# Dummy products placed by the planner, and instruction fetches planned behind the queued data

## The chip, the cores and the metric

The kernel runs on one core of a Trainium2 chip. The metric is the device time of one execution in microseconds (us). PE is TensorE, DVE is VectorE, ACT is ScalarE, POOL is GpSimd, and SP is the engine that issues the loads and stores.

## The reference

Three layers follow each other, in float32. The first is attention in chunks: 4 batches of 8 heads, 768 positions, head size 64. A chunk of 32 queries sees 8 memory keys and the keys of its own chunk, of 16 positions to the left and of 8 to the right. The result, as 3072 tokens of 512 values, goes through two dense blocks:

```python
h = x @ w_in                      # 512 -> 2048
g = h * np.clip(h + 3.0, 0.0, 6.0) / 6.0
x = g @ w_out                     # 2048 -> 512
h = x @ w2_in
g = np.maximum(0.01 * h, h)
out = g @ w2_out
```

## The kernel before

Every dense product is made of three PE products of rounded parts (high times high, high times low, low times high). Weights arrive as 64-bit words; ACT and DVE decode each one into a high and a low part (`decode`, `split_w`), some 3 us of DVE for a weight tile. The tokens are worked on in blocks of 512. The first block is made of attention units: two whole units of 384 tokens (`unit(0, 0)` in the PSUM tile `at`, `unit(0, 1)` in `ab`) and two half units of 192 tokens (`half_unit(1, 0)` in two banks `h`, `half_unit(1, 1)` in `ac`). A unit is a chain: load q, k and v (SP) - windows of k copied (ACT, DVE or POOL) - `scores` (PE, L549 and L816) - `greatest` (DVE) - `exp` (ACT) - `total`, `norm` (DVE) - `transpose` (PE, L607 and L871) - `take_p` (ACT) - `values` (PE, L627, L639, L887, L899; for the first units also behind `memory`, a POOL copy of the memory rows in v) - `hi_x` (ACT) and `lo_x` (DVE), which write the high and low part of the block's `xh` and `xl`. When all four chains have written `xh`, the first dense product (L1003) can start.

The order of the work on each engine is written at build time by a planner, `schedule`. Each piece of work is a `Task` with a key (lower is more urgent), durations by engine, the tasks that it follows, and the tiles that it takes (`allocs`) or uses. The planner steps through a time of its own: whenever an engine is free it takes the most urgent task that is ready there, and emits its instructions. On the chip every engine runs its instructions in that order, each waiting for the data that it needs. The planner also prices loads (issue, start, rate, `LANDS` until the landing is seen, `SURE` as a margin) and, in `feed`, PE's instruction fetch: so many instructions held at the start (`HELD` = 447), so many more by each fetch (`FETCHED` = 256), `FETCH` after it is asked for.

Before the first dense product PE has little to do. `warm` adds tasks of dummy products, `ident` times `ident` (L466), at nine fixed points of the attention: two at the start, then one to three after certain `scores`, `transpose` and `values` tasks. They write the tile `ac`, from 512 columns wide at first to 256 columns later, where `ac` is at the same time the home of the second half unit.

Of the kernel before, what the change touches and what calls it, by code (L numbers as in the profile page):

```python
# [23 lines left out]
QK = 2 * G + 2 * KW  # L24
RAW = QK + 2 * D
NC = G // CHUNK
# [9 lines left out]
N = 512  # L36
# [18 lines left out]
PLAN += [(150 + 12 * k, "2i", k, 430 + 10 * k) for k in range(8)] + [(250 + 12 * k, "2o", k, 520 + 6 * k) for k in range(8)]  # L55
ROOMY = (3, 4, 5)
SOON = 15
RATE_QK, RATE, RATE_V, COLD = 380.0, 220.0, 300.0, 1.1
LOADS = ((-150, -149, -146, -144), (-148, -147, -142, -140), (-145, -138), (-143, -137), (-120, -118), (-116, -114))
WEIGHTS = (-141, -139, -136, -135, -134, -133, -115, -113, -112, -111, -110, -109)  # L60
SHIFT, SHIFT_HALF = (0,), (0,)
# [7 lines left out]
class Task:  # L69


    def __init__(self, fn, opts, key, after=(), allocs=(), uses=(), moe=False, issues=1, late=0, loads=False, ins=8):
        self.late, self.loads, self.ins = late, loads, ins
        self.fn, self.opts, self.key, self.moe, self.issues = fn, opts, key, moe, issues
        self.allocs, self.next, self.left, self.ready = allocs, [], 0, 0.0
        self.bufs = list(allocs) + list(uses)
        self.taken = False
        for b in self.bufs:
            b.users += 1
        for t in after:  # L80
            t.next.append(self)
            self.left += 1
# [9 lines left out]
QUEUED = 6000.0  # L92
LANES = 8
ISSUE = {"SP": 500.0, "POOL": 1000.0}
STARTS, LANDS, SURE = 1900.0, 500.0, 1500.0
HELD, FETCHED, FETCH, STALL = 447, 256, 5000.0, 250.0
AHEAD = 60
OTHER = 20
SLACK = 2500.0
# [1 line left out]
MARGIN = 300.0  # L101


def schedule(tasks, places, ends):

# [4 lines left out]
    future = []  # L112
    events, n, progress, now, wire = [], 0, 0, 0.0, 0.0
    lanes = {e: [0.0] * LANES for e in ISSUE}
    queue = (0, HELD, None)

    def feed(at, task):
        used, held, comes = queue
        for _ in range(task.ins):
            if comes is not None and comes <= at:  # L120
                held, comes = held + FETCHED, None
            if comes is None and used >= held - FETCHED:
                comes = at + FETCH
            if used >= held:
                at, held, comes = comes, held + FETCHED, None
            used += 1
            at += task.opts["PE"] / task.ins
        return at, (used, held, comes)
# [28 lines left out]
                    offer(t)  # L157

    def finish(task, e):
        for b in task.bufs:  # L160
            b.users -= 1
            if b.users == 0:
                live[b.tag].remove(b)
                for w in waiting[b.tag]:
                    offer(w)
                waiting[b.tag].clear()
        for t in task.next:
            if e == "PE" and e in t.opts:
                continue
            t.left -= 1  # L170
            if not t.left:
                push(now + (MARGIN if "PE" in t.opts and not t.moe else 0.0), "ready", t)
# [5 lines left out]
    while events:  # L178
# [10 lines left out]
        while again:  # L189
            again = False  # L190
            for e, h in heaps.items():
# [30 lines left out]
                for item in held:  # L222
                    heapq.heappush(h, item)
                if pick is None:
                    continue
                pick.taken = True
                for b in pick.allocs:
                    live[b.tag].append(b)
                pick.fn(e)
# [6 lines left out]
                if e == "SP" or pick.loads:  # L236
                    at = now
                    for _ in range(pick.issues):
                        at = max(at, lanes[e].pop(0)) + ISSUE[e]
                        wire = max(wire, at + STARTS) + d / pick.issues  # L240
                        lanes[e].append(wire + LANDS)
                    free[e] = at if pick.loads else max(at, wire - QUEUED)
                    push(free[e], "free", None)
                    push(wire + LANDS + (SURE if pick.allocs else 0.0), "done", (pick, e))
                    continue
                if e == "PE":
                    end, queue = feed(now, pick)
# [9 lines left out]
def tile_attn_moe_moe2(ctx: ExitStack, tc: tile.TileContext, raw, w1i, w1o, w2i, w2o, out):  # L257
# [196 lines left out]
    def made(b):  # L454
        return b.t if b.t is not None else make(b)

    marks = {}

    def warm(n, after=None, home=None):

        b, c = home or Buf("ac"), 2 if home else 4

        def fn(e):
            x = made(b)[:, 1, N - 128 * c:].rearrange("p (a n) -> p a n", a=c)
            for _ in range(n):
                nc.tensor.matmul(x, ident, ident.unsqueeze(1).to_broadcast([128, c, 128]), start=True, stop=True, skip_group_check=True)  # L466

        add(fn, {"PE": c * n * (220.0 if after else 430.0)}, after.key + 0.5 if after else -200.0, after=[after] if after else [], allocs=[] if home else [b], uses=[home] if home else [], ins=4 * n)

    def unit(j, quad, key, tag, own=False, direct=False, loads=None):  # L470

# [250 lines left out]
        l2 = [add(load_whole(i) if plain else load_v(i), {"SP": dma(128 * 2 * NC * 512, RATE_V if plain else RATE)}, loads[2 + i], after=() if own else t, allocs=[v[i]], issues=3 if plain else 6, loads=plain) for i in range(2)]  # L722
        if plain:
            l2 = [add(memory(i), {"POOL": 1500.0}, key - 20, after=[l2[i]], uses=[v[i]]) for i in range(2)]
        t = marks["s", j, quad] = add(scores, {"PE": (COLD if direct else 1.0) * 1300.0}, key - 16, ins=192, after=t, allocs=[ps], uses=[*qk, *kw])
        scored = t
        if direct and quad in SHIFT:
            t = add(greatest, {"DVE": 2100.0}, key - 15, after=[t], allocs=[mx, e], uses=[ps])
            t = add(exp_all, {"ACT": act(2 * PAIRS * W)}, key - 13, after=[t], uses=[e])
            t = add(total, {"DVE": 1250.0}, key - 12, after=[t], allocs=[s], uses=[e])  # L730
        else:
            t = add(greatest, {"DVE": 1200.0}, key - 15, after=[t], allocs=[mx], uses=[ps])
            t = add(exp(0), {"ACT": 6 * 330.0}, key - 13, after=[t], allocs=[e, s], uses=[ps, mx])
            if not own:
                turn[:] = [scored] if roomy else [t, *l2]
            t = add(exp(1), {"ACT": 6 * 330.0}, key - 13, after=[t], uses=[ps, mx, e, s])
            t = add(total, {"DVE": 350.0}, key - 12, after=[t], uses=[s])
        t = add(norm, {"DVE": 900.0} if direct else {"POOL": 1800.0, "DVE": 900.0}, key - 11, after=[t], uses=[e, s])
        t = marks["t", j, quad] = add(transpose, {"PE": (COLD if direct else 1.0) * 600.0}, key - 7, ins=12, after=[t], uses=[e, ps])
        t = add(take_p, {"ACT": act(PAIRS * 128)}, key - 5, after=[t], uses=[pt, e])  # L740
        t = marks["v", j, quad] = add(values_whole if plain else values, {"PE": (COLD if direct else 1.0) * 1600.0}, key, ins=192, after=[t, *l2], uses=[e, *v, ps])
        if jb >= PLAIN:
            to_pair(t, key, 0, NU)
            return
# [9 lines left out]
    def half_unit(j, quad, gp, key, tag, loads, copies, cold):  # L754
# [192 lines left out]
            if not blk:  # L947
                behind[:] = [a1]

        l1 = add(load_qk, {"SP": dma(128 * 2 * QK * 4, RATE_QK)}, loads[0], allocs=[qk])  # L950
        l2 = add(load_v, {"SP": dma(128 * 2 * NC * 512, RATE_V)}, loads[1], allocs=[v], issues=4 if whole else 8, loads=not gp)
        if whole:
            l2 = add(memory, {"POOL": 1500.0}, key - 20, after=[l2], uses=[v])
        t = add(windows, {copies: {"ACT": 1050.0, "DVE": 700.0, "POOL": 1800.0}[copies]}, key - 30, after=[l1], allocs=[kw], uses=[qk])
        t = marks["s", j, quad, gp] = add(scores, {"PE": cold * 650.0}, key - 16, ins=96, after=[t], allocs=banks, uses=[qk, kw])
        marks["b", j, quad, gp] = banks
        if gp or quad not in SHIFT_HALF:
            t = add(greatest, {"DVE": 700.0}, key - 15, after=[t], allocs=[mx], uses=banks)
            t = add(exp, {"ACT": 6 * 330.0}, key - 13, after=[t], allocs=[e, s], uses=[*banks, mx])
            t = add(total, {"DVE": 350.0}, key - 12, after=[t], uses=[s])  # L960
        else:
            t = add(greatest, {"DVE": 1250.0}, key - 15, after=[t], allocs=[mx, e], uses=banks)
            t = add(exp_all, {"ACT": act(2 * NC * W)}, key - 13, after=[t], uses=[e])
            t = add(total, {"DVE": 800.0}, key - 12, after=[t], allocs=[s], uses=[e])
        t = add(norm, {"DVE": 500.0}, key - 11, after=[t], uses=[e, s])
        t = marks["t", j, quad, gp] = add(transpose, {"PE": cold * 300.0}, key - 7, ins=6, after=[t], uses=[e, *banks])
        t = add(take_p, {"ACT": act(NC * 128)}, key - 5, after=[t], uses=[*banks, e])
        t = marks["v", j, quad, gp] = add(values_whole if whole else values, {"PE": cold * 900.0}, key, ins=96, after=[t, l2], uses=[e, v, *banks])
        jb, at = divmod(begins, N)
        first = min(2 * G, N - at)  # L970
        to_x(jb, t, key, at, 0, first)
# [590 lines left out]
        unit(0, u, -80.0 + 6.0 * u, ("at", "ab")[u], own=True, direct=True, loads=LOADS[u])  # L1562
    for u in range(2):
        half_unit(1, u, 0, -68.0 + 6.0 * u, ("h", "ac")[u], LOADS[2 + u], ("POOL", "DVE")[u], COLD)
    warm(2)
    warm(1, marks["s", 0, 0])
    warm(2, marks["s", 0, 1])
    warm(1, marks["s", 1, 0, 0])
    home = marks["b", 1, 1, 0][0]
    for m, n in ((("s", 1, 1, 0), 2), (("t", 0, 0), 3), (("t", 0, 1), 3), (("t", 1, 1, 0), 2), (("v", 1, 0, 0), 2)):  # L1570
        warm(n, marks[m], home)
    for u in range(2):
        half_unit(1, u, 1, -20.0 + 6.0 * u, "at", LOADS[4 + u], "ACT", 1.0)
    for u in range(2):
# [62 lines left out]

    with tc.manual_schedule():
        constants()
        schedule(tasks, places, ends)  # L1640

# [49 lines left out]
```

## Time and profile before

| what | value |
|---|---|
| time, median of 3 runs | 1047.82 us (1047.02 to 1048.76) |
| time of the profiled execution | 1049.14 us |
| its span, first to last instruction | 1047.4 us |
| mean granted clock of PE over the span | 0.992 of full |

The span is the stretch that the trace covers; the execution's own time holds 1.7 us more around it. Granted clock 1.00 is PE at 2.4 GHz, 0.50 is 1.2 GHz.

### The profile page before, as it was taken

Reading aid. Unit: us, or ns where it says so; the run is one execution under the profiler, and the core shown is the slowest. Engines: PE = TensorE matmul, PEld = TensorE weight load, DVE = VectorE, ACT = ScalarE, POOL = GpSimd, SP = SyncE. Lnnn points to the kernel's source line nnn. Section 1 sums busy time; section 2 is a strip of 40 time slices with the busy share of each in tenths; the row PEclk is TensorE's granted clock in tenths of the full one; section 3 lists DMA queues with packets and bytes.
Section 4 is the critical chain, followed back from the end, with each engine's and each line's share of the span. In section 5 each row is a group of like instructions: output and inputs, shape, how many; then the busy total and the mean of one; then the engine's idle time right before and its main releaser. Section 6 shows DMA issues by size and latency. Waiting matters only on the chain.

```text
span 1047.4 us, 20225 instructions
## 1 busy us (share of the span) xinstructions
PE 1035.1 (99%) x7476; PEld 850.3 (81%) x7476; DVE 875.3 (84%) x1485; ACT 693.7 (66%) x1480; POOL 20.8 (2%) x30
## 2 busy tenths in 40 slices
PE   7999999999999999999999999999999999999998
PEld 4778988888788888888888888888888888888886
DVE  6898988778998778799999899999576998566775
ACT  4786876655888555476686576785565874666753
POOL 3010000000000000000000000000000000000000
PEclk8899999999999999999999999999999999999999
DMA  9889787876887979673648778546342454423451
GB/s 265 283 216 331 241 291 230 258 229 221 262 282 239 332 225 290 239 239 123 214 144 268 253 251 280 183 158 221 111 171 81 174 193 156 173 109 96 146 181 61
DMA packets 127314, 220.49 MB, mean 211 GB/s; under 512 B 12528, under 2 KB 76016, under 8 KB 127216
## 3 DMA queue, kind: packets, MB, share of 16 engines
q1 hardware_dynamic: 127216, 219.20, 63.9%
q8 instruction: 59, 0.97, 0.4%
q14 instruction: 39, 0.32, 0.1%
HBM read 156.24 MB, written 62.91 MB: 209 GB/s over the span
## 4 chain that ended last, share of the span: by engine, by line
PE 89%; DVE 4%; DMA 3%; ACT 3%; issue 1%; SPq 0%; DVEq 0%; ACTq 0%
PE y L1327 15%; PE y L1052 13%; PE y L1495 12%; PE h L1327 10%; PE h L1495 8%; PE hx L1495 8%; PE h L1003 7%; PE hx L1327 7%; PE h L1052 2%; PE at L639 2%; DMA w<-in_raw 2%; PE at L549 1%; DVE w L345 1%; PE at L607 1%; PE ac L466 1%
## 5 line engine op out<-in xcount | busy, mean ns | idle before, releaser
L345 DVE TENSOR_TENSOR w<-w 128x512 fp32r<-128x512 f32 (+2 forms) x393 | 322.9, 854 | 25.8 <-ACT w L342 23.9
L342 ACT CAST w<-w 128x512 fp32r<-128x512 f32 (+1 forms) x290 | 223.3, 803 | 13.4 <-PE hx L1495 3.6
L1052 PE MATMUL y<-g,w 128*128 128x512 f32 (+1 forms) x540 | 125.2, 375 | 0.9 <-ACT g L342 0.7
L1327 PE MATMUL y<-w 128*128 128x512 f32 x516 | 124.6, 390 | 0.0
L1327 PEld LDWEIGHTS y<-w 128*128 128x128 f32 x516 | 96.6, 188 | 20.1
L1052 PEld LDWEIGHTS y<-g,w 128*128 128x128 f32 x540 | 94.1, 189 | 19.0 <-ACT g L342 1.2
L342 ACT CAST g<-w 128x512 fp32r<-128x512 f32 x80 | 49.4, 620 | 63.8 <-PE y L1495 23.0
L1495 PE MATMUL y<-w 128*128 128x512 f32 x384 | 90.3, 389 | 0.0
L1495 PEld LDWEIGHTS y<-w 128*128 128x128 f32 x384 | 72.1, 188 | 14.9
L1301 ACT ACTIVATE w<-w 128x512 f32<-128x512 f32 x72 | 45.0, 630 | 40.4 <-DVE w L1372 18.1
L1003 PE MATMUL h<-xh,w 128*128 128x512 f32 (+1 forms) x288 | 66.1, 370 | 0.5 <-DVE w L345 0.5
L345 DVE TENSOR_TENSOR g<-w,g 128x512 fp32r<-128x512 f32 x80 | 54.1, 684 | 14.3 <-ACT g L342 14.2
L1495 PE MATMUL h<-w 128*128 128x512 f32 x264 | 62.1, 389 | 0.0
L1495 PE MATMUL hx<-w 128*128 128x512 f32 x252 | 59.2, 389 | 0.0
L1327 PE MATMUL h<-xl,w 128*128 128x512 f32 x240 | 58.3, 391 | 0.0
L1495 PEld LDWEIGHTS h<-w 128*128 128x128 f32 x264 | 49.6, 188 | 10.3
L1003 PEld LDWEIGHTS h<-xh,w 128*128 128x128 f32 x288 | 49.7, 189 | 9.9 <-DVE w L345 0.9
L1495 PEld LDWEIGHTS hx<-w 128*128 128x128 f32 x252 | 47.3, 188 | 9.8
L1327 PEld LDWEIGHTS h<-xl,w 128*128 128x128 f32 x240 | 44.8, 188 | 9.9 <-DVE xl L345 0.4
L1327 PE MATMUL y<-xh,w 128*128 128x512 f32 x216 | 52.2, 390 | 0.0
L1327 PEld LDWEIGHTS y<-xh,w 128*128 128x128 f32 x216 | 40.5, 188 | 8.4
L1052 PE MATMUL y<-w 128*128 128x512 f32 x180 | 46.6, 391 | 0.0
(244 smaller groups left out, 1852.2 us busy)
## 6 DMA issues: line engine op xcount, KB each, us to landing
w<-kept2i SPq DMA_DIRECT2D x42, 512.0 KB
w<-kept2o SPq DMA_DIRECT2D x42, 512.0 KB
w<-kept1i SPq DMA_DIRECT2D x28, 512.0 KB
a<-in_raw SPq DMA_DIRECT2D x20, 448.0 KB
w<-in_w1i SPq DMA_DIRECT2D x16, 512.0 KB
w<-in_w1o SPq DMA_DIRECT2D x16, 512.0 KB
w<-in_w2i SPq DMA_DIRECT2D x16, 512.0 KB
w<-in_w2o SPq DMA_DIRECT2D x16, 512.0 KB
```

Source lines behind the costliest of these rows:

```text
L342: nc.scalar.copy(out, in_) if e == "ACT" else engine(e).tensor_copy(out=out, in_=in_)
L345: engine(e).tensor_tensor(out=out, in0=a, in1=b, op=ALU.subtract)
L466: nc.tensor.matmul(x, ident, ident.unsqueeze(1).to_broadcast([128, c, 128]), start=True, stop=True, skip_group_check=True)
L549: nc.tensor.matmul(ps.t[h * CHUNK:(h + 1) * CHUNK, par, i * W:(i + 1) * W], qk[h // 2].t[r, gp, (h % 2) * G + c * CHUNK:(h % 2) * G + (c + ...
L607: nc.tensor.transpose(pt.t[:, i // NC, (i % NC) * 128:(i % NC + 1) * 128], pview()[:, i * 128:(i + 1) * 128], ident)
L639: nc.tensor.matmul(pv.t[(h % 2) * D:(h % 2 + 1) * D, par, (h // 2) * 2 * G + i * CHUNK:(h // 2) * 2 * G + (i + 1) * CHUNK], v[h // 2].t[r, ...
L1003: nc.tensor.matmul(h.t[:, o:o + n], w.t[:, 1 if p == 1 else 0, k * 128:(k + 1) * 128], x[:, k, c0:c0 + n], start=(p == 0 and k == 0 and o ...
L1052: nc.tensor.matmul(bank(banks[d])[:, c0:c0 + n], w.t[:, 1 if p == 1 else 0, d * 128:(d + 1) * 128], g.t[:, 1 if p == 2 else 0, at:at + n], ...
L1301: return add(lambda e: nc.scalar.activation(out=at(), in_=at(), func=AF.Prelu, alpha=0.01), {"ACT": act(N)}, key, after=[after], uses=uses)
L1327: nc.tensor.matmul(bank(to), wt(l, o)[:, kt * 128:(kt + 1) * 128].bitcast(F32R), operand(p, name, 1 if q == 2 else 0, kt).bitcast(F32R), s ...
L1495: nc.tensor.matmul(bank(to[d]), wt(1 if q == 1 else 0, o)[:, d * 128:(d + 1) * 128].bitcast(F32R), g.t[:, 1 if q == 2 else 0], start=(fres ...
```

## The change

The fixed `warm` tasks go. In their place the planner puts in a dummy product itself, whenever PE is free in its time, no task is ready, no dense product has been taken yet (`not progress`), and a bank is open. A bank is open from when the task marked `opens` has finished (its readers are done) until a task marked `closes` is taken, which writes it next. Dummies are 64 columns wide, priced at 230 ns, until the planner's time is 3.5 us, and 512 columns wide, priced at 880 ns, after that. A dummy counts 4 instructions.

The planner's prices change too. A load that allocates a tile is now believed seen 0.5 us after its last byte where it is issued in the planner's first 20 us (before: 2.0 us), and 1.75 us later on (before: 2.0 us). The v loads of the first units are priced at 240 instead of 300 bytes a ns, the q and k loads of the first half units at 300 instead of 380. A fetch of instructions is asked for when 40 of those held are used (before: 191), and comes 2.5 us behind the last byte of the data queued by then, at the latest 8 us after it is asked for (before: 5 us after it).

```diff
-RATE_QK, RATE, RATE_V, COLD = 380.0, 220.0, 300.0, 1.1
+RATE_QK, RATE, RATE_V, COLD = 380.0, 220.0, 240.0, 1.1
...
-STARTS, LANDS, SURE = 1900.0, 500.0, 1500.0
-HELD, FETCHED, FETCH, STALL = 447, 256, 5000.0, 250.0
+STARTS, LANDS, SURE, SOONER, MOST = 1900.0, 250.0, (250.0, 1500.0), 20000.0, 8000.0
+HELD, FETCHED, ASKS, FETCH, STALL = 447, 256, 407, 2500.0, 250.0
+FIRST, LATER, FIRST_TILL = (64, 230.0), (512, 880.0), 3500.0
...
-            if comes is None and used >= held - FETCHED:
-                comes = at + FETCH
+            if comes is None and used >= held - ASKS:
+                comes = min(max(at, max((y for x, y in queued if x <= at), default=0.0)) + FETCH, at + MOST)
...
     def finish(task, e):
+        if task.opens:
+            spots.append(task.opens)
...
                 if pick is None:
+                    if e == "PE" and not progress and spots:
+                        cols, took = FIRST if now < FIRST_TILL else LATER
+                        filler(spots[0], cols)
+                        fill = Task(None, {"PE": took}, 0, ins=4)
+                        end, queue = feed(now, fill)
+                        free[e] = end
+                        push(end, "free", None)
                     continue
                 pick.taken = True
+                for b in pick.closes:
+                    if b in spots:
+                        spots.remove(b)
...
-                    push(wire + LANDS + (SURE if pick.allocs else 0.0), "done", (pick, e))
+                    push(wire + LANDS + (SURE[now > SOONER] if pick.allocs else 0.0), "done", (pick, e))
...
+    begun_at = Buf("ac")
+
+    def filler(b, cols):
+        t = made(b)
+        nc.tensor.matmul((t[:, 1] if b.tag[0] == "a" else t)[:, N - cols:], ident, ident.unsqueeze(1).to_broadcast([128, cols // 128, 128]) if cols > 128 else ident[:, :cols], start=True, stop=True, skip_group_check=True)
...
-    warm(2)
-    warm(1, marks["s", 0, 0])
-    warm(2, marks["s", 0, 1])
-    warm(1, marks["s", 1, 0, 0])
-    home = marks["b", 1, 1, 0][0]
-    for m, n in ((("s", 1, 1, 0), 2), (("t", 0, 0), 3), (("t", 0, 1), 3), (("t", 1, 1, 0), 2), (("v", 1, 0, 0), 2)):
-        warm(n, marks[m], home)
```

In the units, `opens` is set on the last reader of the scores (`greatest` or `exp`) and on `take_p`, `closes` on `transpose` and `values`, and on the `scores` of the half unit in `ac` for the bank that is open at the start.

## Rows read from the trace of the kernel before

**Rows 1.** The page's head: span, and busy us of each engine.
```profile
span 1047.4 us, 20225 instructions
...
PE 1035.1 (99%) x7476; PEld 850.3 (81%) x7476; DVE 875.3 (84%) x1485; ACT 693.7 (66%) x1480; POOL 20.8 (2%) x30
```

**Rows 2.** Windows: length, busy us by engine (instructions), clock, DMA share, GB/s.
```profile
200.00:400.00 200.00, 199.30 (x1692) 163.19 (x1691) 164.99 (x300) 132.38 (x333) 4.69 (x3) 1.00 0.79 258
...
1000.00:1048.00 48.00, 43.47 (x192) 35.67 (x190) 32.24 (x47) 22.11 (x36) 0.00 (x0) 0.99 0.33 116
```

**Rows 3.** PE in order of time, first 40 us: start, us, line, operation, [idle before].
```profile
1.36 3.78 PE L466 MATMUL ac<-ident 128*128 128x512 f32 x4 [1.36 <-POOL three L308]
...
6.28 1.46 PE L549 MATMUL at<-w 64*32 64x64 f32 x92 [0.25 <-DVE w L342]
...
10.11 1.99 PE L466 MATMUL ac<-ident 128*128 128x512 f32 x4
...
12.62 0.35 PE L816 MATMUL h<-w 64*32 64x64 f32 x17 [0.28 <-POOL w L342]
14.37 0.45 PE L816 MATMUL h<-w 64*32 64x64 f32 x29 [1.40 <-issue]
...
17.28 1.51 PE L607 MATMUL at<-ident,w 128*128 128x128 f32 x6
18.72 2.93 PE L466 MATMUL ac<-ident 128*128 128x256 f32 x6
23.62 2.08 PE L466 MATMUL ac<-ident 128*128 128x256 f32 x4 [1.97 <-ACT w L850]
25.62 2.97 PE L627 MATMUL at<-w 64*64 64x32 f32 x96
28.52 1.54 PE L607 MATMUL ab<-ident,w 128*128 128x128 f32 x6
...
38.21 0.98 PE L887 MATMUL ac<-w 64*64 64x32 f32 x48
...
39.77 0.50 PE L1003 MATMUL h<-xh,w 128*128 128x512 f32 x1
```

**Rows 4.** Windows of 1 us, columns as in rows 2.
```profile
15.00:16.00 1.00, 0.87 (x2) 0.04 (x1) 0.49 (x3) 1.00 (x9) 0.00 (x0) 0.97 0.98 346
16.00:17.00 1.00, 0.96 (x48) 0.85 (x48) 1.00 (x3) 0.19 (x2) 0.00 (x0) 0.50 1.20 311
...
33.00:34.00 1.00, 1.00 (x37) 0.83 (x37) 0.00 (x0) 0.72 (x2) 0.00 (x0) 0.99 0.23 69
```

**Rows 5.** Windows from the first windows copy to PE's wait at 78.65.
```profile
5.80:39.77 33.97, 29.85 (x672) 21.50 (x672) 24.59 (x68) 16.12 (x65) 9.58 (x16) 0.75 0.91 272
39.77:78.65 38.88, 37.15 (x389) 28.72 (x383) 37.80 (x83) 34.00 (x114) 2.79 (x2) 1.00 0.85 246
```

**Rows 6.** Waits of PE over the span: waiter, releaser, us, times, longest.
```profile
PE h L1003 <- DVE w L345: 0.5, 1, 0.5
```

**Rows 7.** All waits of DVE from 20 to 40 us.
```profile
DVE xl L345 <- ACT xh L342: 2.9, 1, 2.9
DVE wm L400 <- ACT wm L397: 2.1, 1, 2.1
DVE mx L862 <- ACT w L850: 1.6, 1, 1.6
```

**Rows 8.** The other engines in order of time, first 40 us.
```profile
9.12 0.96 DVE L566 TENSOR_REDUCE mx<-at 128x12 f32<-128x768 f32 x1
...
20.80 1.18 DVE L867 TENSOR_TENSOR w<-w,mx 128x384 f32<-128x384 f32 x1
...
21.68 0.31 ACT L850 ACTIVATE w<-ac,mx 128x64 f32<-128x64 f32 x1 [2.00 <-PE ac L466]
...
24.12 0.57 DVE L867 TENSOR_TENSOR w<-w,mx 128x384 f32<-128x384 f32 x1
...
24.69 1.55 POOL L342 COPY w<-w 8x768 f32<-8x768 f32 x2 [0.41 <-DMA w<-in_raw]
```

More of the change, by code (lines that the diff above doesn't have):

```diff
@@ L69, with __init__ @@
 class Task:
-    def __init__(self, fn, opts, key, after=(), allocs=(), uses=(), moe=False, issues=1, late=0, loads=False, ins=8):
-        self.late, self.loads, self.ins = late, loads, ins
+    def __init__(self, fn, opts, key, after=(), allocs=(), uses=(), moe=False, issues=1, late=0, loads=False, ins=8, opens=None, closes=()):
+        self.late, self.loads, self.ins, self.opens, self.closes = late, loads, ins, opens, closes
         self.fn, self.opts, self.key, self.moe, self.issues = fn, opts, key, moe, issues
@@ L101, with schedule @@
 MARGIN = 300.0
-def schedule(tasks, places, ends):
+def schedule(tasks, places, ends, filler, spots):
     free = {"PE": 0.0, "DVE": 0.0, "ACT": 0.0, "POOL": 0.0, "SP": 0.0}
@@ L114, in schedule @@
     lanes = {e: [0.0] * LANES for e in ISSUE}
-    queue = (0, HELD, None)
+    queue, queued = (0, HELD, None), []
     def feed(at, task):
@@ L241, in schedule @@
                         lanes[e].append(wire + LANDS)
+                        queued.append((at, wire))
+                    del queued[:-40]
                     free[e] = at if pick.loads else max(at, wire - QUEUED)
                     push(free[e], "free", None)
-                    push(wire + LANDS + (SURE if pick.allocs else 0.0), "done", (pick, e))
+                    push(wire + LANDS + (SURE[now > SOONER] if pick.allocs else 0.0), "done", (pick, e))
                     continue
@@ L455, in made @@
         return b.t if b.t is not None else make(b)
[L457 to L468, printed above, removed]
+    begun_at = Buf("ac")
+    def filler(b, cols):
+        t = made(b)
+        nc.tensor.matmul((t[:, 1] if b.tag[0] == "a" else t)[:, N - cols:], ident, ident.unsqueeze(1).to_broadcast([128, cols // 128, 128]) if cols > 128 else ident[:, :cols], start=True, stop=True, skip_group_check=True)
     def unit(j, quad, key, tag, own=False, direct=False, loads=None):
@@ L724, in unit @@
             l2 = [add(memory(i), {"POOL": 1500.0}, key - 20, after=[l2[i]], uses=[v[i]]) for i in range(2)]
-        t = marks["s", j, quad] = add(scores, {"PE": (COLD if direct else 1.0) * 1300.0}, key - 16, ins=192, after=t, allocs=[ps], uses=[*qk, *kw])
+        t = add(scores, {"PE": (COLD if direct else 1.0) * 1300.0}, key - 16, ins=192, after=t, allocs=[ps], uses=[*qk, *kw])
         scored = t
         if direct and quad in SHIFT:
-            t = add(greatest, {"DVE": 2100.0}, key - 15, after=[t], allocs=[mx, e], uses=[ps])
+            t = add(greatest, {"DVE": 2100.0}, key - 15, after=[t], allocs=[mx, e], uses=[ps], opens=ps)
             t = add(exp_all, {"ACT": act(2 * PAIRS * W)}, key - 13, after=[t], uses=[e])
@@ L735, in unit @@
                 turn[:] = [scored] if roomy else [t, *l2]
-            t = add(exp(1), {"ACT": 6 * 330.0}, key - 13, after=[t], uses=[ps, mx, e, s])
+            t = add(exp(1), {"ACT": 6 * 330.0}, key - 13, after=[t], uses=[ps, mx, e, s], opens=ps)
             t = add(total, {"DVE": 350.0}, key - 12, after=[t], uses=[s])
         t = add(norm, {"DVE": 900.0} if direct else {"POOL": 1800.0, "DVE": 900.0}, key - 11, after=[t], uses=[e, s])
-        t = marks["t", j, quad] = add(transpose, {"PE": (COLD if direct else 1.0) * 600.0}, key - 7, ins=12, after=[t], uses=[e, ps])
-        t = add(take_p, {"ACT": act(PAIRS * 128)}, key - 5, after=[t], uses=[pt, e])
-        t = marks["v", j, quad] = add(values_whole if plain else values, {"PE": (COLD if direct else 1.0) * 1600.0}, key, ins=192, after=[t, *l2], uses=[e, *v, ps])
+        t = add(transpose, {"PE": (COLD if direct else 1.0) * 600.0}, key - 7, ins=12, after=[t], uses=[e, ps], closes=[ps])
+        t = add(take_p, {"ACT": act(PAIRS * 128)}, key - 5, after=[t], uses=[pt, e], opens=ps)
+        t = add(values_whole if plain else values, {"PE": (COLD if direct else 1.0) * 1600.0}, key, ins=192, after=[t, *l2], uses=[e, *v, ps], closes=[ps])
         if jb >= PLAIN:
@@ L948, in to_x @@
                 behind[:] = [a1]
-        l1 = add(load_qk, {"SP": dma(128 * 2 * QK * 4, RATE_QK)}, loads[0], allocs=[qk])
+        l1 = add(load_qk, {"SP": dma(128 * 2 * QK * 4, RATE_QK if gp else 300.0)}, loads[0], allocs=[qk])
         l2 = add(load_v, {"SP": dma(128 * 2 * NC * 512, RATE_V)}, loads[1], allocs=[v], issues=4 if whole else 8, loads=not gp)
@@ L954, in half_unit @@
         t = add(windows, {copies: {"ACT": 1050.0, "DVE": 700.0, "POOL": 1800.0}[copies]}, key - 30, after=[l1], allocs=[kw], uses=[qk])
-        t = marks["s", j, quad, gp] = add(scores, {"PE": cold * 650.0}, key - 16, ins=96, after=[t], allocs=banks, uses=[qk, kw])
-        marks["b", j, quad, gp] = banks
+        t = add(scores, {"PE": cold * 650.0}, key - 16, ins=96, after=[t], allocs=banks, uses=[qk, kw], closes=[begun_at] if banks[0].tag == "ac" else ())
         if gp or quad not in SHIFT_HALF:
             t = add(greatest, {"DVE": 700.0}, key - 15, after=[t], allocs=[mx], uses=banks)
-            t = add(exp, {"ACT": 6 * 330.0}, key - 13, after=[t], allocs=[e, s], uses=[*banks, mx])
+            t = add(exp, {"ACT": 6 * 330.0}, key - 13, after=[t], allocs=[e, s], uses=[*banks, mx], opens=banks[-1])
             t = add(total, {"DVE": 350.0}, key - 12, after=[t], uses=[s])
         else:
-            t = add(greatest, {"DVE": 1250.0}, key - 15, after=[t], allocs=[mx, e], uses=banks)
+            t = add(greatest, {"DVE": 1250.0}, key - 15, after=[t], allocs=[mx, e], uses=banks, opens=banks[-1])
             t = add(exp_all, {"ACT": act(2 * NC * W)}, key - 13, after=[t], uses=[e])
@@ L965, in half_unit @@
         t = add(norm, {"DVE": 500.0}, key - 11, after=[t], uses=[e, s])
-        t = marks["t", j, quad, gp] = add(transpose, {"PE": cold * 300.0}, key - 7, ins=6, after=[t], uses=[e, *banks])
-        t = add(take_p, {"ACT": act(NC * 128)}, key - 5, after=[t], uses=[*banks, e])
-        t = marks["v", j, quad, gp] = add(values_whole if whole else values, {"PE": cold * 900.0}, key, ins=96, after=[t, l2], uses=[e, v, *banks])
+        t = add(transpose, {"PE": cold * 300.0}, key - 7, ins=6, after=[t], uses=[e, *banks], closes=banks[:1])
+        t = add(take_p, {"ACT": act(NC * 128)}, key - 5, after=[t], uses=[*banks, e], opens=banks[0])
+        t = add(values_whole if whole else values, {"PE": cold * 900.0}, key, ins=96, after=[t, l2], uses=[e, v, *banks], closes=banks)
         jb, at = divmod(begins, N)
@@ L1639, in tile_attn_moe_moe2 @@
         constants()
-        schedule(tasks, places, ends)
+        schedule(tasks, places, ends, filler, [begun_at])
 def kernel(**inputs):
```

## The prediction

> **What bounds the kernel now.** I read the page's head first, then windows of the whole span, then PE in order of time, and only then the waits. The head says that PE is busy for 1035.1 of 1047.4 us [rows 1], so there are some 12 us in which PE does nothing, and more in which what it does is worth nothing. The windows say where these are not: of the five long stretches between 100 and 1000 us the worst leaves PE 0.70 us idle, and the 4.5 us at the end are the stores behind the last product [rows 2]. So whatever the change can win lies in the first 100 us.
>
> There PE runs nine groups of dummies between the pieces of attention, and the first dense product comes at 39.77 [rows 3]. Three things go wrong on the way. PE runs out of instructions at 12.97 and stands for 1.40 us, released by "issue", which is no engine's data. Soon afterwards the granted clock falls from 1.00 to 0.50, and it is back only at 33 [rows 4]: at 1.2 GHz transposes take 1.51 and `values` 2.97 us. And the dummies in `ac` stand in line with the half unit that lives there: its `exp` waits 2.00 us for six of them [rows 8], and the next four wait 1.97 us for that `exp` [rows 3]. So `values` of the first unit runs at 25.62.
>
> What does that delay cost? The last input of the first block is a v tile, whose memory rows POOL writes from 24.69 to 26.24 [rows 8]. `values` takes 0.98 us and the first product now starts 0.58 us behind the last `values` [rows 3]: 26.24 + 0.98 + 0.58 = 27.8. PE could be 12.0 us earlier. But the stretch behind belongs to DVE: from 39.77 to 78.65 it is busy for 37.80 of 38.88 us, PE for 37.15 [rows 5], and PE's one wait for a decoded weight ends that stretch [rows 6]. PE drains a lead there until DVE holds it up. The gain is therefore what DVE wins in its own time, not what PE wins.
>
> **The change part by part.** *The fixed dummies go, and no dummy stands any more in a bank that is still read.* DVE sat idle from 20 to 40 us in three waits: 2.9 us for `xh`, which waited for the late `values`; 2.1 us for the first step of a decode, which stood on ACT behind a `take_p` that waited for the late transposes; 1.6 us for the `exp` that the dummies held up [rows 7]. All three come from PE's lateness: together 6.6 us. If transposes and `values` run when their inputs are there, all of it goes: -6.6. The bounds: nothing, if PE stays as late as it is; and 33.97 - 24.59 = 9.4 us, all that DVE idles before 39.77 [rows 5]. I take 6.6, as the 2.8 us beside it are waits for loads and for the first scores, which the change does not feed faster.
>
> *Dummies now come wherever the planner sees a gap.* A wide one is two products; they take 0.50 us each at full clock and 0.95 at half [rows 3]. Ahead of the first `scores` the planner puts 3.5/0.23 = 16 narrow ones and, as its own loads and windows copies come to about 6.6 us, four wide ones. At the planned prices that is 1.36 + 3.7 + 3.5 = 8.6 us on the trace's clock, where the scores start at 6.28 now. DVE reads them at 9.12 [rows 8], 1.4 us after they end, which covers most of it; 0.9 is left, some of it in waits that DVE has anyway. Bounds 0 and 0.9 in this case (more is a rival); I take +0.6. Later on, a real piece waits for the dummy in front, at worst 1.0 us, on average half of one. DVE has decodes to do meanwhile, so this hardly adds up: bounds 0 and 1.0, I take +0.5.
>
> *DVE gets denser beside POOL.* The 128x384 product L867 took 1.18 us while POOL copied, and 0.57 us elsewhere [rows 8]: 0.6 us each time that a DVE instruction meets such a copy. With the copies where they are and DVE fuller there, one or two more may meet: bounds 0 and 1.2, I take +0.6. The Trainium skill (SBUF — State Buffer, the section on the ports) says that DVE with two SBUF inputs and POOL take a shared pair of ports in turn, for whole instructions; that row agrees. By that rule alone every such pair would collide, and this term would stand at its upper bound.
>
> *The fetch.* Narrow dummies use instructions early, so that a fetch is asked for early. The 1.40 us stall itself lies before a half unit's scores that DVE first reads some 3 us later, so its own worth in the sum is nothing; its worth is the clock, which is in the three waits above. *The prices of loads and rates* move the order of everything behind the start a little. PE's idle time there, under 1 us in 900, bounds a gain; I bound a loss by the same and take 0.
>
> The sum: -6.6 + 0.6 + 0.5 + 0.6 = -4.9. Against the profiled execution's 1049.14 that gives 1044.2. The median of the runs shown is 1.3 below that execution, so the forecast is 1042.9.
>
> **The rivals.** *PE runs dry earlier and the clock falls again.* By 12.97 PE had issued two units' scores of 96 products, ten products of dummies and 19 of the half unit's scores, 221 with as many weight loads: 442 instructions, near the 447 that the planner counts as held. Sixteen dummies of 4 instead of the first two wide ones add about 56, so it runs dry near the second scores, at about 10. If the fetch lands no earlier than at 14.37, the stall is over 4 us with no dummy in it. Then the clock is low again for a while and PE pays for transposes and `values`: 1.51 + 2.97 + 1.54 = 6.0 us for what takes half of that at full clock, so 3.0 of the gain go: 1045.9. For it speaks that a fall followed a stall of 1.40; against it, that the fetch is asked for earlier and that dummies fill every gap behind it. By the Trainium skill (Runtime: NRT & Kernel Launch, the section on instruction fetch), the next block is fetched while the current one runs and the cost is mostly hidden; by that rule this rival would have no chance. The stall in [rows 3] says otherwise, and I go by it.
>
> *The loads keep their old times.* DMA is at a share of 0.91 up to 39.77 and 0.85 behind [rows 5]. If DVE meets weights that have not landed where it waits for PE today, its 6.6 us are only renamed: 1047.8. Against it: loads of the first block's successors wait for tiles that `scores` and `values` set free, and those come earlier.
>
> *The early dummies cost more than their price (slower).* They run before the clock is up. A wide one then takes 1.9, not 0.88. A narrow one has no row: by its columns it takes 64/512 of that, 0.24; by the transposes' 128 columns, 1.54/6 each, two take 0.51. Then 16 narrow and four wide ones end between 1.36 + 3.8 + 3.5 = 8.7 and 1.36 + 8.2 + 7.6 = 17.2 us. DVE's chain starts later by as much, less its 1.4 us of cover: up to 9.5 us, against 6.6 - 1.1 = 5.5 won later. It decides from first scores at 6.28 + 1.4 + 5.5 = 13.2 us on, and at its end gives 1047.8 + 4.0 = 1051.8. Against it: with two wide ones at the start, products take 0.50 us by 10.11 [rows 3], and data that land at 24.69 forgive some of it.
>
> **How the numbers follow.** The sum has 0.60, and its own range is 1040.5 to 1045. PE dry again: 0.17. Loads at their old times: 0.12. Early dummies too dear: 0.11. About 0.2%, or 2.1 us, is what a measurement can tell from no change. Faster by more: 0.60 and about two thirds of the 0.17, together 0.71. Within it: the rest of that and the loads, 0.18. Slower: 0.11. The range reaches down to 1039.0, near 1047.8 - 9.4 = 1038.4 where DVE loses no time at all, and up to 1047.4, which takes in PE running dry and part of the loads' case; the slower rival and the rest of the loads' are left out.
>
> **What would show it.** Right: no L466 in front of an `exp`, the granted clock at 1.00 from the start to 39 us, `values` of the first unit before 20, the first dense product at 29 to 33, DVE's three waits gone, and in exchange more waits of PE for DVE (L345) before 75, since DVE then sets the pace. PE meets that wait at about 73 to 75 instead of 78.65. From 100 us on all should be the same, moved by some 5 us. Wrong: first scores behind 10 us; a gap of PE ended by "issue" of over 2 us; a clock of 0.50 behind 16; DVE idle for loads where it idled for PE; or PE early at 30 and the same time at the end, which would say that the stretch behind the start has another limit than DVE.

## The result and the profile after

The changed kernel took 1061.32 us (median of 5 runs, 1057.64 to 1061.97) against 1047.82 us: ratio 1.0117, 95% interval 1.0097 to 1.0137. It is slower by 13.5 us, where 4.9 us faster was forecast. The profiled execution is one of the shorter ones, 1057.64 us.

The page's head, span and busy us by engine:

```profile
span 1055.8 us, 20289 instructions
...
PE 1038.3 (98%) x7502; PEld 853.3 (81%) x7502; DVE 878.3 (83%) x1487; ACT 694.2 (66%) x1478; POOL 22.2 (2%) x30
```

Against [rows 1] PE is busy 3.2 us longer in a span that is 8.4 us longer: idle time, dummies and products at a low clock. PE in order of time shows the start:

```profile
1.36 12.03 PE L476 MATMUL ac<-ident 128*128 128x64 f32 x40 [1.36 <-POOL three L323]
13.31 1.17 PE L557 MATMUL at<-w 64*32 64x64 f32 x96
...
15.47 1.17 PE L557 MATMUL ab<-w 64*32 64x64 f32 x83
19.44 0.34 PE L557 MATMUL ab<-w 64*32 64x64 f32 x13 [2.81 <-issue]
...
39.16 0.32 PE L895 MATMUL h<-w 64*64 64x32 f32 x3 [1.71 <-issue]
...
42.90 3.23 PE L1010 MATMUL h<-xh,w 128*128 128x512 f32 x8
```

The first scores come at 13.31 instead of 6.28 us [rows 3], and the first dense product at 42.90 instead of 39.77. Groups of PE's products up to 16 us, shapes apart (busy us, mean ns of one), say what the dummies cost:

```profile
L476 PE MATMUL ac<-ident 128*128 128x64 f32 x32 | 7.1, 423 | 1.4 <-POOL three L323 1.4
L476 PE MATMUL ac<-ident 128*128 128x512 f32 x10 | 6.3, 771 | 0.0
```

Sixteen narrow dummies are 32 products that start every 0.21 us, so one costs 0.43 us where the planner prices it at 0.23. They end at 8.24, and the four wide ones fill the time to 13.31: 1.27 us each at a price of 0.88, as their products last 1.06 us each until 10.9 us and 0.59 from 11.5 on. Waits of DVE in the first 20 us:

```profile
DVE w L357 <- DMA w<-in_raw: 6.3, 3, 5.4
DVE at L571 <- PE at L557: 5.9, 1, 5.9
DVE ab L571 <- PE ab L557: 3.3, 1, 3.3
```

Before, DVE waited there for loads alone. Of the three waits of [rows 7] 0.6 us is left, for `xh`; two for PE's scores, 9.2 us together, stand in their place. From 100 us on most of the loss shows: windows (columns as in rows 2), then the longest waits of PE in that stretch (us, times, longest).

```profile
100.00:200.00 100.00, 97.74 (x1596) 83.58 (x1595) 84.39 (x173) 73.90 (x251) 3.35 (x2) 1.00 0.79 249
200.00:400.00 200.00, 195.82 (x1673) 159.40 (x1672) 170.69 (x310) 131.12 (x331) 7.54 (x4) 1.00 0.81 261
```

```profile
PE y L1059 <- ACT ys L1089: 1.7, 2, 0.9
PE h L1334 <- ACT xl L357: 1.2, 1, 1.2
PE at L557 <- issue: 1.2, 2, 0.7
PE at L557 <- DVE xl L360: 0.8, 1, 0.8
PE at L615 <- POOL a L611: 0.6, 1, 0.6
```

PE idles 6.44 us from 100 to 400 us; before it was 0.81, 0.70 of it in the window of [rows 2]. In that window POOL takes four tasks instead of three. No dummy is put in there: the code between is the same, but the planner took its tasks in another order.

### The profile page after: what moved, and what is told of

Same layout as the page of the kernel before. It is cut to its first block, busy times and chain, and to the rows that moved or that the text cites. A ratio compares the mean times of both kernels' runs of the same rounds, so it can differ in the third digit from the quotient of the medians.

```text
span 1055.8 us, 20289 instructions
## 1 busy us (share of the span) xinstructions
PE 1038.3 (98%) x7502; PEld 853.3 (81%) x7502; DVE 878.3 (83%) x1487; ACT 694.2 (66%) x1478; POOL 22.2 (2%) x30
## 4 chain that ended last, share of the span: by engine, by line
PE 84%; DVE 9%; DMA 2%; ACT 2%; issue 2%; POOL 0%; SPq 0%; ACTq 0%; DVEq 0%; POOLq 0%
PE y L1334 13%; PE y L1502 12%; PE y L1059 12%; PE h L1334 9%; PE h L1502 8%; PE hx L1334 8%; PE hx L1502 8%; PE h L1010 7%; PE h L1059 2%; DVE w L360 2%; PE ac L476 1%; PE at L647 1%; DMA kept2i<-ys 1%; PE at L557 1%; DVE w L1362 1%
## 5 line engine op out<-in xcount | busy, mean ns | idle before, releaser
L1334 PE MATMUL y<-w 128*128 128x512 f32 x516 | 124.2, 389 | 0.0
L1502 PE MATMUL y<-w 128*128 128x512 f32 x384 | 90.3, 389 | 0.0
L1010 PE MATMUL h<-xh,w 128*128 128x512 f32 (+1 forms) x288 | 68.4, 376 | 0.6 <-ACT xh L357 0.3
L360 DVE TENSOR_TENSOR g<-w,g 128x512 fp32r<-128x512 f32 x80 | 54.3, 686 | 11.5 <-ACT g L357 11.4
L1502 PEld LDWEIGHTS h<-w 128*128 128x128 f32 x264 | 49.6, 188 | 10.3
L1379 DVE TENSOR_TENSOR w<-y,w 128x512 f32<-128x512 f32 x35 | 23.9, 688 | 32.3 <-PE y L1334 26.1
```

The source lines that it names most:

```text
L360: engine(e).tensor_tensor(out=out, in0=a, in1=b, op=ALU.subtract)
L1010: nc.tensor.matmul(h.t[:, o:o + n], w.t[:, 1 if p == 1 else 0, k * 128:(k + 1) * 128], x[:, k, c0:c0 + n], start=(p == 0 and k == 0 and o ...
L1334: nc.tensor.matmul(bank(to), wt(l, o)[:, kt * 128:(kt + 1) * 128].bitcast(F32R), operand(p, name, 1 if q == 2 else 0, kt).bitcast(F32R), s ...
L1379: done[2] = add(lambda e: nc.vector.tensor_tensor(out=half_of(x, 0), in0=bank(bb), in1=ut.t[:, 0], op=ALU.add), low, key, after=[k, done[1 ...
L1502: nc.tensor.matmul(bank(to[d]), wt(1 if q == 1 else 0, o)[:, d * 128:(d + 1) * 128].bitcast(F32R), g.t[:, 1 if q == 2 else 0], start=(fres ...
```

## The experiments

Two causes were put against each other: the dear dummies ahead of the first scores ("the head"), and the order in which the planner, with other prices, takes the tasks behind ("the order"). "Lateness" is how much later than before the dense products start that stood at the given time in the trace of before (negative: earlier), one profiled execution each. The trace of before is 1.3 us above the median of before, so that a lead or lateness of that size at the end says less than the medians do. In the traces of e1, e5, e6, e9 and e10 PE, DVE, ACT and POOL run their instructions in the order of before, dummies aside and but for one pair of products that change places in e9; in the others the order is another.

| run | median us | before, same chip | ratio, 95% interval | lateness at 39.8 | 103.7 | 113.9 | 331 | 999.8 |
|---|---|---|---|---|---|---|---|---|
| changed kernel | 1061.32 | 1047.82 | 1.0097 to 1.0137 | 3.1 | 0.2 | 3.9 | 10.8 | 8.9 |
| e1, dummies of the head alone | 1054.01 | 1047.09 | 1.0040 to 1.0081 | 7.7 | 7.4 | 7.2 | 7.3 | 6.9 |
| e2, light head | 1057.43 | 1047.09 | 1.0077 to 1.0116 | -3.9 | -5.1 | 2.6 | 7.8 | 5.8 |
| e3, one dummy | 1059.24 | 1047.09 | 1.0105 to 1.0135 | -3.5 | -3.5 | 4.5 | 12.0 | 10.0 |
| e4, old prices | 1054.67 | 1047.09 | 1.0056 to 1.0086 | 2.5 | 1.4 | 2.9 | 7.9 | 6.6 |
| e5, before, no shared bank | 1049.10 | 1047.94 | 1.0004 to 1.0026 | -4.0 | -2.9 | -1.7 | -1.6 | -1.7 |
| e6, before, five groups of dummies out | 1048.87 | 1047.94 | 0.9993 to 1.0012 | -4.6 | -2.7 | -2.4 | -2.4 | -2.0 |
| e7, before, load prices | 1049.28 | 1047.94 | 1.0000 to 1.0025 | -5.7 | 4.9 | 5.3 | 6.4 | 4.5 |
| e8, before, fetch price | 1051.95 | 1047.94 | 1.0023 to 1.0051 | -4.5 | 3.0 | 1.6 | 4.4 | 2.5 |
| e9, old order frozen | 1053.45 | 1047.97 | 1.0040 to 1.0070 | 2.8 | 4.5 | 4.5 | 4.5 | 4.6 |
| e10, as e9, wide at the head | 1047.15 | 1047.97 | 0.9983 to 1.0003 | -2.9 | -0.7 | -0.1 | 0.3 | -0.2 |
| e11, before, one price off by 50 ns | 1057.63 | 1047.97 | 1.0075 to 1.0113 | -2.8 | -0.8 | 0.7 | 8.2 | 6.5 |
| e12, changed kernel again | 1061.97 | 1047.97 | 1.0122 to 1.0152 | 4.9 | 2.9 | 6.6 | 15.0 | 13.0 |

**The head in the old order (e1).** The kernel before, with the changed kernel's 16 narrow and four wide dummies ahead of the first scores.

```diff
+            if after is None:
+                for _ in range(16):
+                    nc.tensor.matmul(b.t[:, 1, N - 64:], ident, ident[:, :64], start=True, stop=True, skip_group_check=True)
+                for _ in range(4):
+                    nc.tensor.matmul(x, ident, ident.unsqueeze(1).to_broadcast([128, c, 128]), start=True, stop=True, skip_group_check=True)
+                return
```

> The kernel before, its order of tasks and its prices untouched; only the two wide dummies at its head become the 16 narrow and 4 wide ones that the changed kernel has there. Theory H (the head: early dummies cost twice their price and the lateness stays to the end): first scores at about 13.3 us instead of 6.28, first dense product some 3 to 7 us later than 39.8, time 1054 to 1061. Theory R (the order behind the start, above all from 100 to 400 us, is what costs): first scores at 13.3 as well, but most of it is forgiven by the loads that land until 24.7 us; PE idle from 100 to 400 us stays near 0.8 us and the time is 1048 to 1052.

PE in order of time:

```profile
1.36 7.09 PE L467 MATMUL ac<-ident 128*128 128x64 f32 x32 [1.36 <-POOL three L308]
8.24 6.11 PE L469 MATMUL ac<-ident 128*128 128x512 f32 x8
14.28 1.17 PE L555 MATMUL at<-w 64*32 64x64 f32 x96
...
47.47 2.18 PE L1009 MATMUL h<-xh,w 128*128 128x512 f32 x8
```

The first scores are 8.0 us late, the first dense product 7.7, and 6.9 are left at 1000 us. Only 0.8 us of the lateness is taken up on the way.

**The head taken out of the changed kernel (e2, e3).** e2 emits two wide dummies at the head and none of the planner's next eighteen; e3 emits one narrow dummy and no other. The planner's prices and order stay.

```diff
+        heads.append(cols)
+        if 2 < len(heads) <= 20:
+            return
+        cols = 512
```
```diff
+        heads.append(cols)
+        if len(heads) > 1:
+            return
```

> The changed kernel with its own order of tasks; of the 20 dummies ahead of the first scores only two (both wide) are emitted, as in the kernel before; all later dummies stay. Theory H: first scores at 6 to 8 us, first dense product before 36 us, time at or below 1048. Theory R: the start comes back by some 3 to 5 us, but PE still idles about 6 us from 100 to 400 us: 1052 to 1057.

> The changed kernel with its own order of tasks, with only one narrow dummy left (the planner still counts time for all of them, but no other is emitted). If dummies keep the clock up and that is worth time, the clock is at 0.50 for most of 10 to 40 us and the time is 1 to 4 us above that of the light head; if the dummies cost more than the clock gives back, it is the same or lower. Theory H and R as for the light head: at or below 1048, or 1052 to 1058.

The first dense products come 3.9 and 3.5 us earlier than before, and both runs are still 10 and 12 us slower, a little more than theory R had. In e2 a lead of 5.1 us becomes a lateness of 2.6 in one place, PE in order of time and a window over it:

```profile
106.75 1.65 PE L1016 MATMUL h<-xh,w 128*128 128x256 f32 x6 [2.25 <-ACT xh L357]
108.86 1.61 PE L563 MATMUL at<-w,a 64*32 64x64 f32 x96 [0.46 <-DVE xl L360]
```
```profile
106.00:113.00 7.00, 5.79 (x114) 5.36 (x115) 6.92 (x17) 4.90 (x17) 0.00 (x0) 0.53 0.38 111
```

PE takes the dense products of the next block when their `xh` is not made, stands 2.25 us, and runs most of the next 7 us at 1.2 GHz. The head alone does not make the loss.

e3 is 1.8 us slower than e2, as expected if dummies keep the clock up, though the intervals of the two overlap a little. The second unit's transposes, PE in order of time in e2 and then in e3:

```profile
20.93 0.88 PE L621 MATMUL ab<-ident,w 128*128 128x128 f32 x6
```
```profile
22.37 1.54 PE L620 MATMUL ab<-ident,w 128*128 128x128 f32 x6
```

Without dummies they take as long as those at 1.2 GHz in [rows 3, 4]. The windows of e3 have the clock at 1.00 there, but its trace holds no clock record before 39.59 us.

**The parts of the change one by one (e4, e7, e8).** e4 is the changed kernel with the old prices and the old fetch rule, so the dummies alone; e7 the kernel before with the new load prices, e8 with the new fetch rule.

```diff
+STARTS, LANDS, SURE, SOONER, MOST = 1900.0, 500.0, (1500.0, 1500.0), 20000.0, 8000.0
...
+            if comes is None and used >= held - FETCHED:
+                comes = at + 5000.0
```
```diff
+STARTS, LANDS, SURE, SOONER = 1900.0, 250.0, (250.0, 1500.0), 20000.0
...
+                    push(wire + LANDS + (SURE[now > SOONER] if pick.allocs else 0.0), "done", (pick, e))
```
```diff
+            if comes is None and used >= held - ASKS:
+                comes = min(max(at, max((y for x, y in queued if x <= at), default=0.0)) + FETCH, at + MOST)
```

> The changed kernel with the prices of loads and of the instruction fetch as in the kernel before: only the dummies are placed by the planner. Theory H: the head is the same as in the changed kernel, first scores at 13 us or later, time 1056 to 1062. Theory R: the order behind the start is a third one, so PE's idle time from 100 to 400 us is another than 6.4 us, and the time moves with it, by up to 5 us either way of 1058.

> The kernel before with only the new prices of the loads (landing, margin, rates); dummies and fetch as before. Theory R (every re-planning changes the order behind the start, and orders differ by several us): first dense product within 2 us of 39.8, PE idle from 100 to 400 us above 0.8 us, time 1048 to 1054. Theory H alone: within 2 us of before, since the head is the same.

> The kernel before with only the new price of the instruction fetch. Theory R: the order behind the start is another, time 1048 to 1054, with PE idle from 100 to 400 us above 0.8 us. Theory H alone: within 2 us of before. If pricing the fetch right is worth something, PE's stall of 1.40 us at 13 us is filled and the first dense product is not later.

The medians are 7.6, 1.3 and 4.0 us above those of before; e7's interval begins at 1.0000, so its 1.3 us is hardly told from nothing. PE idles 3.02, 1.30 and 3.82 us from 100 to 400 us. e4 stays under the 1056 us of theory H, and with the old prices it still falls 5.0 us behind between 113.9 and 331 us: the dummies too, by the time that they take in the plan, give another order. e7's runs spread from 1046.56 to 1053.20 and its profile fell on the longest, so its lateness is that of a bad execution. e7 and e8 emit no dummy that the kernel before lacks and have their first dense product 5.7 and 4.5 us early (e7 was expected within 2 us); what they lose after that comes with the other order. In e8 the stall at 13 us shrinks from 1.40 to 0.18 us, as hoped, and the time is longer all the same.

**The cure alone, in the old order (e5, e6).** e5 puts the five dummies that stand around the half unit's `exp` (ten products, six in front of it and four behind) into `ab` instead; e6 leaves out all five late groups. The rest is the kernel before.

```diff
+        marks["p", j, quad] = ps
...
-        warm(n, marks[m], home)
+        warm(n, marks[m], marks["p", 0, 1] if m in (("s", 1, 1, 0), ("t", 0, 0)) else home)
```
```diff
-            for _ in range(n):
+            for _ in range(0 if home else n):
```

> The kernel before, its order and prices untouched; the dummies behind the scores of the second half unit and behind the first transposes (five of 256 columns) are written to the bank pair ab, which nobody reads then, instead of ac. Theory H (what PE gains or loses in the start stays to the end, as the head alone showed): both waits of 2.0 us go, the first dense product comes 2 to 4 us earlier and the time falls by 1.5 to 4 us, to about 1044. Theory D (the prediction's: the stretch behind the start belongs to DVE): DVE's waits of 1.6 and part of 2.9 us go, about the same time. Rival: the lead is lost at the next wait of PE for DVE, 78 us, and the time is within 1 us of before.

> The kernel before, its order and prices untouched; the five groups of dummies that write ac while it is the half unit's home are not emitted, those ahead of it stay. Theory H: PE has 9 to 10 us less to do between 17 and 39 us and both waits of 2.0 us go; transposes and values still run at half clock, so the first dense product comes at 31 to 36 us and the time falls by 3 to 8 us. If the clock is what these dummies are worth, then it is still at 0.50 when the dense products begin, these run at half rate for some us, and half of that gain is lost: 1043 to 1046.

The 2.0 us waits of [rows 3, 8] are gone, the first dense product comes 4.0 and 4.6 us earlier, and the time does not fall, against theory H (e5, e6) and theory D (e5). All waits of DVE from 20 to 40 us, which were 6.6 us in [rows 7], e5 and then e6:

```profile
DVE xl L345 <- ACT xh L342: 2.3, 1, 2.3
```
```profile
DVE xl L345 <- ACT xh L342: 1.7, 1, 1.7
```

Longest waits of PE, e5 and then e6:

```profile
PE at L817 <- ACT w L342: 1.9, 1, 1.9
PE ac L888 <- issue: 1.7, 1, 1.7
```
```profile
PE ac L887 <- issue: 4.8, 1, 4.8
```

A PE that is early runs out of instructions between 28 and 34 us, for 4.83 us in e6. Of its lead of 4.6 us e6 gives 1.6 back in the first ten dense products, at 1.2 GHz, and 1.0 at two more stalls for instructions, at 85 and 103 us. What is left at 1000 us is 1.7 and 2.0 us in the profiles, and nothing in the medians.

**The changed kernel in the old order (e9, e10).** In e9 each engine takes its tasks in the order of the kernel before, from a list; only where dummies go is the planner's. e10 also makes the head's dummies 512 wide at a price of 1.72 us and takes the old fetch rule, which here moves dummies only.

```diff
+    follow = {e: [tasks[int(i)] for i in v.split()][::-1] for e, v in ORDER_OF.items()}
...
+                line, pick = follow[e], None
+                if line and getattr(line[-1], "offered", False) and blocked(line[-1]) is None:
+                    pick = line.pop()
```
```diff
-FIRST, LATER, FIRST_TILL = (64, 230.0), (512, 880.0), 3500.0
+FIRST, LATER, FIRST_TILL = (512, 1720.0), (512, 880.0), 3500.0
```

> The changed kernel with its dummies and its new prices, but every engine takes its tasks in the order of the kernel before (only where dummies go is still the planner's). Theory A (two causes: the late first scores cost about 7 us, and the order that the planner finds with the new prices costs the rest): TensorE's idle time from 100 to 400 us falls from 6.4 us back to about 1 us, and the time is that of the first experiment, 1051 to 1056 us. Theory B (the head alone makes the loss, whatever the order behind it): the time stays with the changed kernel, 1057 to 1062 us.

> As the ninth, with dummies at the head 512 columns wide and priced at 1.72 us each (the changed kernel: 64 columns at 0.23 us), and the old fetch rule. Theory A: first scores at 5 to 7 us, the first dense product within 2 us of 39.77 us, idle time from 100 to 400 us about 1 us, time 1045 to 1050 us, level with the kernel before or a little under it. Theory B gives the same here. A theory that the dummies behind the head are what costs: over 1053 us.

Windows of e9 show the idle time back at 1.58 us (0.89 + 0.69):

```profile
100.00:200.00 100.00, 99.11 (x1513) 85.08 (x1512) 85.80 (x175) 74.67 (x245) 2.95 (x2) 1.00 0.81 256
200.00:400.00 200.00, 199.31 (x1782) 163.07 (x1781) 164.96 (x298) 132.91 (x334) 4.70 (x3) 1.00 0.78 253
```

So 8.5 us (1061.97 - 1053.45) are the order's. The head is what is left: with five wide dummies there, and as many dummies behind it as in e9, the time is 6.3 us less. The two don't simply add up: the head costs 6.9 us in the old order (e1), but 3.2 in the new one (13.5, less the 10.3 that e2 still loses). e10 in order of time:

```profile
1.36 7.58 PE L460 MATMUL ac<-ident 128*128 128x512 f32 x10 [1.36 <-POOL three L307]
8.87 1.17 PE L541 MATMUL at<-w 64*32 64x64 f32 x96
...
33.45 1.10 PE L879 MATMUL ac<-w 64*64 64x32 f32 x24 [3.42 <-issue]
35.52 1.46 PE L808 MATMUL at<-w 64*32 64x64 f32 x48 [0.98 <-ACT w L341]
36.91 3.78 PE L994 MATMUL h<-xh,w 128*128 128x512 f32 x8
```

The scores are later than the 5 to 7 us expected, and the dense product still 2.9 us early. A stall of 3.42 us for instructions comes first, then the clock is at 0.50, and eight products take 3.78 us that took 2.18 in e1: 1.7 of the 2.9 us are given back by 51 us. e10 ends level with the kernel before; no run beat it beyond the uncertainty.

**A price that means nothing (e11), and the changed kernel again (e12).**

```diff
-STARTS, LANDS, SURE = 1900.0, 500.0, 1500.0
+STARTS, LANDS, SURE = 1900.0, 450.0, 1500.0
```

> The kernel before with one price moved by 50 ns (a load's landing 450 instead of 500 ns): dummies, fetch rule and every other line as before. Theory A's second half (a greedy planner's order is a draw: any price moved gives another one, and the order of the kernel before is among the good ones): the time moves by some us, up rather than down, 1049 to 1055 us, and PE idles 2 to 7 us more from 100 to 400 us. Its rival (only prices that are wrong do harm): within 1 us of the kernel before.

> The changed kernel once more, to see whether its two times (1057.7 and 1061.5 us in the runs on record) are two places of a clock fall. Theory: a profile of the longer kind shows a second stretch at a granted clock under 0.7 between 100 and 120 us, where the second unit's input comes just in time; a profile of the shorter kind shows none. Rival: the longer kind differs in the first 40 us alone, by when the instruction packets land.

50 ns in one price cost 9.7 us, with the dummies and the fetch rule of before; 1 to 7 were expected. PE idles 5.63 us from 100 to 400 us, and waits longest, over the span, in these places:

```profile
PE y L1052 <- ACT w L342: 3.6, 1, 3.6
...
PE h L1327 <- ACT xl L342: 1.8, 1, 1.8
```

e12 fell on the longer kind of execution. The clock fall that I expected at 100 to 120 us isn't there (1.00 throughout), and the rival holds only in part. PE in order of time, and a window:

```profile
20.25 0.34 PE L557 MATMUL ab<-w 64*32 64x64 f32 x13 [3.66 <-issue]
...
43.09 1.46 PE L824 MATMUL at<-w 64*32 64x64 f32 x48 [2.51 <-ACT w L357]
...
151.93 0.96 PE L557 MATMUL at<-w,a 64*32 64x64 f32 x71 [1.98 <-issue]
```
```profile
20.00:25.00 5.00, 4.75 (x27) 1.64 (x34) 4.09 (x8) 2.89 (x20) 1.72 (x4) 0.66 0.70 184
```

The stall in the second scores is 3.66 us instead of 2.81, behind it the clock is down, a wait for ACT of 2.51 us follows, and one more stall at 150 us is 1.98 instead of 0.72. Against the shorter execution e12 is 1.8 us later at the first dense product, 2.7 by 58 us and 4.1 by 190, so less than half of the difference arises in the first 40 us. What decides between the kinds was not tried.

## Why the prediction was wrong

**"The prices of loads and rates ... I take 0."** This is the step that failed most: the term measured 8.5 us and not 0. I bounded a loss by the idle time there before, under 1 us; that is what the found order leaves, not what another order can cost. With the order put back the changed kernel is 8.5 us faster (e9), with a light head it still loses 10.3 us (e2), and one price off by 50 ns loses 9.7 (e11). The 8.5 us are not the prices' alone, as the dummies reorder too (e4). The planner is greedy: each of the three edits of prices tried in the kernel before (e7, e8, e11) gave another sequence, and none was faster than that of before. Which waits make one order worse than another was not traced to its cause.

**"I take +0.6" for the early dummies.** The mechanism was the slower rival's, with a chance of 0.11: first scores at 13.31 us, where it was to decide from 13.2. The term measured 7.0 us at the first scores and 6.3 (e10 against e9) to 6.9 us (e1) at the end. A wide dummy measured 1.27 us, between the 0.88 and the 1.9 of that rival. Of the two bounds for a narrow dummy, 0.24 by its columns and 0.51 by the transposes, the second is near the 0.43 measured.

**"But the stretch behind belongs to DVE."** DVE is the busier engine from 39.77 to 78.65 us, but that share did not make it a buffer: 7.7 us of lateness pass to the end as 6.9 (e1). Nor does a lead end there: e6 is 3.4 us early on both sides of PE's wait for the decoded weight, which is 0.5 us as in [rows 6]. So "data that land at 24.69 forgive some of it" fails too.

**"All of it goes: -6.6."** DVE did win 4.3 us (e5) and 4.9 (e6) of it, and PE did win 4.0 us (e5), 4.6 (e6) and 2.9 (e10) at the first dense product, not the 12.0 that the v tile would allow. But at 1000 us 0.2 to 2.0 are left in those profiles, and the medians show no gain. The next limit in those runs is PE's instructions: stalls of 1.7, 4.8 and 3.4 us between 28 and 34 us, in all three followed by products at 1.2 GHz. That PE would be faster with the fetch out of the way was not tried, since no edit here moves it without moving PE's work.

**PE running dry** came as that rival counted it, in the second scores (15.47 + 1.17 us), but at 16.6 us instead of 10 and for 2.81 to 3.66 us instead of over 4. The Trainium skill (Runtime: NRT & Kernel Launch, the section "Instruction fetch mechanics") has the fetch mostly hidden. The traces differ: each kernel here has a stall that "issue" ends, the longest of each 0.9 (e11) to 4.83 us (e6).

**"DVE gets denser beside POOL"**, +0.6, can't be told from the time here; a product of two inputs is stretched by 0.6 us beside POOL once in the trace of before (1.18 us, [rows 8]) and once in that of the changed kernel (1.59 us at 22.56, 0.96 at 27.29). Of the text's own signs of being wrong, first scores behind 10 us and a gap of over 2 us ended by "issue" both came; "From 100 us on all should be the same" failed too.

## What to carry to other kernels

When a planner with a greedy choice orders the work, a change of a price is two changes: what it says, and another order. Freeze the old order to cost the first, and move some unrelated price by a trifle to see how wide the draw of the second is, before an edit is believed or thrown away. Idle time that a good order leaves bounds what can be gained there, never what can be lost.

## What the runs showed of the hardware

- A product of 64 columns with 128 x 128 weights starts every 0.21 us in the first 8 us, and two make a dummy: 0.43 us, where a wide dummy of eight times the columns takes 1.27 right behind. By its columns, from the 0.95 us that each product of 512 columns takes at the start in [rows 3], a narrow one would be 0.24. Narrow dummies are no cheap filler.
- The first instruction packet goes by about the 191st instruction of PE, not by the 40th as the new rule has it. It starts at 11.58 (before), 16.76 (changed), 18.61 (e1), 16.75 (e9) and 13.71 us (e10): 4.1, 2.9, 3.8, 2.6 and 4.0 us behind the 191st, but 4.8 to 13.1 us behind the 40th. The count itself isn't pinned: in the traces any from 150 to 203 spreads as little. In the changed kernel the 40th is used at 5.47 us, and PE stands until 19.44.
- Getting PE to its work earlier lengthens its stalls for instructions: up to the first dense product they are 1.40 us before, and 0.62, 0.88 and 4.83 us where five groups of dummies are left out (e6).
